# Eight retention units ahead of the first gated product, with its weights prepared in small steps

## The chip, the cores and the metric

The kernel runs on one core of a Trainium2 chip. The core has five engines that follow their own instruction streams in order and wait for each other through semaphores: TensorE (PE, matmuls, whose weight loads are listed as PEld), VectorE (DVE), ScalarE (ACT), GpSimd (POOL) and SyncE (SP, which issues all DMAs here). The metric is the device time of one execution in microseconds; each program was timed in several runs and the median counts. One further execution was taken with the hardware profiler, and all rows below are from that one.

## What is computed

Retention (attention with a decaying mask, no softmax) over 8 batches, 8 heads and 576 positions, then two feed-forward layers on the 4608 tokens.

```python
def _attn_ref(q, k, v):                        # (8, 8, 576, 64)
    scores = scale * np.matmul(q, k.transpose(0, 1, 3, 2))
    Dmat = np.where(rel >= 0, gamma[:, None, None] ** rel[None, :, :], 0.0)
    ret = scores * Dmat[None, :, :, :]
    return np.matmul(ret, v)

def _moe_ref(x, w_in, w_out):                  # 512 -> 2048 -> 512
    h = x @ w_in
    g = h * np.cos(h)
    return g @ w_out

def _moe2_ref(x, w1, w2, w3, w_out):           # 512 -> 768 -> 512
    h = np.maximum(np.maximum(x @ w1, x @ w2), x @ w3)
    return h @ w_out
```

## The kernel before

The tokens are cut into 9 blocks of 512 (`NBLK`), the heads into 4 pairs (`NPAIR`), so retention has 36 units, numbered n = 4 x block + pair; a tile `u1_2` belongs to block 1, pair 2, unit 6. A unit loads 1 MB of q, k and v (`att_load`), scales v on POOL (`att_scale`), multiplies q and k on PE (`att_scores`, `sc`, 16 small matmuls), masks the scores on DVE (`att_mask`), adds k and v products to a running state in PSUM (`att_state`, one matmul for each chunk of up to 128 positions), copies the state to SBUF on ACT before each of them (`att_keep`), forms the output on PE from masked scores and copied states (`att_out`, `po`), and decays it on DVE into the block's quarters `k1`, `k2` (`att_decay`). All pairs keep their state in one PSUM bank, so a state matmul follows the last copy out of that bank.

The matrix products use a seven-product scheme on quarters of the matrices, and each operand is split in a high and a low part: seven products of 12 matmuls take the place of eight. `build_in` prepares a block's seven operands `x_x` (differences of quarters, the high part as a cast on ACT, the low part as a subtraction on DVE). A group (`group_in`) does the seven products (`d_a`, `b_a`, `sums` are its PSUM banks) for two weight pairs; its last product is written after four products of the next group. The result goes through `gate` (h cos h) on ACT and DVE. In the first phase each block has two groups, with weight pairs 0 and 1, then 2 and 3; a second phase does the other half with operands stored to DRAM and loaded again as `x_y`.

Weights come as 64-bit floats. For each pair the raw halves are loaded, `widen` (ACT, two activations a half) and `join` (DVE, two instructions a half) build the single-precision value, `total` (POOL) adds its two parts to `fa`, `sums` (DVE, four instructions) forms differences of quarters, `piece_high` casts on ACT and `piece_low` subtracts on DVE. `lead_in` does this for pairs 0 to 3 in the opening: five steps, one a slot, both halves in one step, the sums and all casts of a pair in the fourth (`add_up`, with `split_pair`). `background` prepares later pairs the same way.

What sets the order is a hand-made agenda. `at(n, fn)` puts a step n slots ahead; `tick()` writes all steps of the current slot, in the order in which they were put there, and goes to the next. Each product of a group ends with a tick, so in the gated phase a slot is one product plus the steps due. The opening runs 15 slots without products (lines 733 to 747). The first five units start two slots apart there (scores at the start, one state step in each following slot, output in the fifth, decay in the sixth); pair 0 starts in slot 0, pair 1 in slot 2, pairs 2 and 3 in slots 12 and 15. From the first product on, a unit starts every 3.5 slots (`start_of`). Every engine executes in written order, and a DMA is written to SP's stream where `at` puts it.

## Time and profile before

| | us |
|---|---|
| median of three runs (lowest, highest) | 1456.78 (1455.54, 1458.35) |
| the profiled execution | 1458.0 |
| span of its instructions | 1456.2 |
| PE busy | 1416.6 (97%) |
| DVE busy | 1166.9 (80%) |
| ACT busy | 779.5 (54%) |
| POOL busy | 177.2 (12%) |

The page gives busy times of the whole span. Where an engine is the bound in one stage and not in another, the windows by stage show it: for each stretch the busy time of each engine with its number of instructions, the clock that was granted to PE as a share of full speed, and the mean busy share of the 16 DMA engines. The timeline lists an engine's instructions in order, equal ones that follow each other in one row, with start, duration, and in square brackets the idle time before the row and what ended it.

### The profile page before, as it was taken

The numbers are of one execution on the slowest core, as the hardware profiler recorded it, in microseconds if no ns is written. First come the engines' busy times: TensorE is split into PE (matmuls) and PEld (weight loads), VectorE is DVE, ScalarE is ACT, GpSimd is POOL, SyncE is SP. The second block draws the span as 40 slices with busy tenths as digits, with TensorE's granted clock in tenths as the row PEclk, the third lists the DMA queues.
The fourth block names the chain that finished last, engine by engine and source line by source line (L and its number), as shares of the span: only waits on it lengthen the run. The fifth ranks groups of instructions, "written<-read, shape, count | busy, mean of one in ns | idle before, by whom it ended". The sixth has DMA issues, their size and how long they took to land.

```text
span 1456.2 us, 26320 instructions
## 1 busy us (share of the span) xinstructions
PE 1416.6 (97%) x10492; PEld 1300.9 (89%) x10492; DVE 1166.9 (80%) x1649; ACT 779.5 (54%) x1259; POOL 177.2 (12%) x128
## 2 busy tenths in 40 slices
PE   7799999999899998999999999999999999999998
PEld 5688888998899998999999999998888888888887
DVE  6877888889887679999999999677676667868875
ACT  3566655666788776454444444344343434545543
POOL 2243343442021000000000000000000000000000
PEclk9999999999999999999999999999999999999999
DMA  7588898996999885456556656923344294535633
GB/s 304 176 286 293 316 309 286 335 329 231 359 379 375 325 301 202 143 184 209 195 190 224 223 185 257 369 72 124 98 147 146 73 348 179 181 117 173 227 121 116
DMA packets 95034, 331.52 MB, mean 228 GB/s; under 512 B 9408, under 2 KB 17600, under 8 KB 88768
## 3 DMA queue, kind: packets, MB, share of 16 engines
q1 hardware_dynamic: 94912, 329.85, 63.9%
q8 instruction: 82, 1.34, 0.4%
q14 instruction: 40, 0.33, 0.1%
HBM read 197.69 MB, written 132.12 MB: 226 GB/s over the span
## 4 chain that ended last, share of the span: by engine, by line
PE 90%; DVE 4%; DMA 2%; ACT 1%; issue 1%; POOL 0%; SPq 0%; POOLq 0%; DVEq 0%; ACTq 0%
PE wo L853 24%; PE d_a L394 13%; PE d_e L415 13%; PE b_e L415 6%; PE b_a L394 6%; PE d_u L1255 4%; PE a_e L415 3%; PE sums L394 3%; PE state L597 3%; PE po L613 3%; PE sc L554 2%; PE b_u L1255 2%; PE po L625 2%; PE d_b L394 2%; DMA x_y<-xs 1%; PE a_u L1255 1%
## 5 line engine op out<-in xcount | busy, mean ns | idle before, releaser
L853 PE MATMUL wo<-h_g,w_wo 128*128 128x256 f32 x1728 | 312.8, 283 | 0.0
L853 PEld LDWEIGHTS wo<-h_g,w_wo 128*128 128x128 f32 x1728 | 269.5, 192 | 0.0
L853 PE MATMUL wo<-l_g,w_wo 128*128 128x256 f32 x864 | 245.1, 284 | 4.6 <-DVE l_g L826 4.5
L853 PEld LDWEIGHTS wo<-l_g,w_wo 128*128 128x128 f32 x864 | 165.8, 192 | 5.6 <-DVE l_g L826 5.4
L394 PE MATMUL d_a<-x_x,w_wi 128*128 128x256 f32 x864 | 120.6, 290 | 1.9 <-DVE x_x L373 1.9
L510 DVE SCALAR_TENSOR_TENSOR s_a<-t_a,s_a 128x1024 f32<-128x1024 f32 x72 | 95.2, 1322 | 28.2 <-ACT t_a L507 28.2
L415 PE MATMUL d_e<-h_e,w_b 128*128 128x512 f32 x432 | 115.5, 389 | 0.0
L394 PEld LDWEIGHTS d_a<-x_x,w_wi 128*128 128x128 f32 x864 | 108.7, 193 | 5.7 <-DVE x_x L373 2.1
L394 PE MATMUL d_a<-x_y,w_wi 128*128 128x256 f32 x864 | 111.6, 285 | 2.1 <-DMA x_y<-xs 2.0
L821 ACT CAST h_g<-tb_g 128x1024 fp32r<-128x1024 f32 x36 | 37.8, 1051 | 139.5 <-DVE tb_g L365 139.5
L394 PEld LDWEIGHTS d_a<-x_y,w_wi 128*128 128x128 f32 x864 | 107.7, 194 | 2.5 <-ACT ar_wo L174 2.1
L440 ACT ACTIVATE ext<-d_e 128x512 f32<-128x512 f32 x72 | 43.0, 597 | 118.2 <-PE d_e L415 117.8
L501 DVE SCALAR_TENSOR_TENSOR t_a<-s_a,t_a 128x1024 f32<-128x1024 f32 x72 | 92.0, 1278 | 17.6 <-ACT t_a L497 17.4
L507 ACT ACTIVATE t_a<-t_a 128x1024 f32<-128x1024 f32 x72 | 76.1, 1056 | 40.0 <-DVE t_a L501 39.8
L415 PEld LDWEIGHTS d_e<-h_e,w_b 128*128 128x128 f32 x432 | 81.0, 188 | 16.8
L186 POOL TENSOR_TENSOR fa_b<-raw_b 128x512 uint32<-128x512 uint32 x18 | 22.2, 1231 | 537.1 <-DVE raw_b L180 499.4
L497 ACT ACTIVATE t_a<-s_a 128x1024 int32<-128x1024 f32 x72 | 76.1, 1057 | 2.1 <-PE d_a L394 1.4
L597 PE MATMUL state<-u 128*128 128x128 f32 (+1 forms) x256 | 56.5, 309 | 15.8 <-ACT u L581 10.9
L444 DVE TENSOR_TENSOR ext<-ext,b_e 128x512 f32<-128x512 f32 x36 | 24.7, 685 | 57.4 <-PE b_e L415 57.4
L581 ACT COPY u<-state 128x128 f32<-128x128 f32 x128 | 32.4, 266 | 67.6 <-PE state L597 67.4
L415 PE MATMUL d_e<-l_e,w_b 128*128 128x512 f32 x216 | 66.5, 389 | 0.0
L597 PEld LDWEIGHTS state<-u 128*128 128x128 f32 (+1 forms) x256 | 39.8, 197 | 25.3 <-issue 11.5
(268 smaller groups left out, 3281.7 us busy)
## 6 DMA issues: line engine op xcount, KB each, us to landing
u<-att SPq DMA_DIRECT2D x36, 1024.0 KB, 8.1
gq<-s_a SPq DMA_DIRECT2D x72, 512.0 KB, 6.9
k_g<-gq SPq DMA_DIRECT2D x72, 512.0 KB, 6.1
xs<-x_x SPq DMA_DIRECT2D x63, 512.0 KB, 8.3
x_y<-xs SPq DMA_DIRECT2D x63, 512.0 KB, 7.5
w_b<-st_b SPq DMA_DIRECT2D x9, 1792.0 KB, 10.7
st_b<-p_b SPq DMA_DIRECT2D x27, 512.0 KB, 4.7
mqp<-ext SPq DMA_DIRECT2D x24, 512.0 KB, 3.1
```

Source lines behind the costliest of these rows:

```text
L394: nc.tensor.matmul(h[:, p * HB : (p + 1) * HB], a, b, start=first and p == 0 and i == 0, stop=i == len(terms) - 1, skip_group_check=True,)
L415: nc.tensor.matmul(dst, a, b, start=first and i == 0, stop=i == len(terms) - 1, skip_group_check=True)
L440: nc.scalar.activation(dst, b[:, :n], AF.Copy, scale=scale)
L497: nc.scalar.activation(st["t"], s, AF.Copy, bias=0.25)
L501: nc.vector.scalar_tensor_tensor(out=r, in0=s, scalar=MOST_TURNS, in1=st["t"], op0=ALU.min, op1=ALU.subtract)
L507: nc.scalar.activation(r, r, AF.Sin, scale=TURN, bias=HALF_PI)
L510: nc.vector.scalar_tensor_tensor(out=s, in0=f32(st["t"]), scalar=-1.0, in1=s, op0=ALU.max, op1=ALU.mult)
L597: nc.tensor.matmul(state[:, hp * CH : (hp + 1) * CH], kn[p : p + m, sl], v[p : p + m, sl], start=False, stop=True, skip_group_check=True,)
L613: nc.tensor.matmul(po[64 * e : 64 * e + 64, s * CH : (s + 1) * CH], v[:, s * CH + 64 * e : s * CH + 64 * e + 64], u["ret"][:, e, s * CH : ...
L821: nc.scalar.copy(h, o[pairs[k][2]])
L853: nc.tensor.matmul(b[:, mt * HB : (mt + 1) * HB], a, v, start=first and mt == 0 and p == 0 and i == 0, stop=last and p == len(ws) - 1 and ...
L1255: nc.tensor.matmul(dst, a, v, start=first and p == 0 and i == 0 and (wide or mt == 0), stop=p == 2 and i == 2, skip_group_check=True,)
```

## The change

Eight units instead of five are started ahead of the first product, two slots apart from slot 1, and the opening runs 17 slots (`LEAD`). From then on a unit starts every 3.75 slots. `at` takes a flag, and steps with it (scores and outputs) are written ahead of the other steps of their slot, so ahead of the state matmuls. The steps of a weight pair are eleven instead of five: each half is widened, joined and totalled by itself, the sums stand alone, and high and low pieces come in two parts each; the list `EARLY` gives their slots (the first pieces are cast a slot before the sums, which they don't need). Pairs 0 to 3 start in slots 0, 3, 12 and 16. Unit 0 is loaded ahead of the first raw weights, and units 0 to 3 and the raw weights of pairs 0 and 1 are asked for at once; the raw weights of pairs 2 and 3 are loaded by halves in slots 8, 9, 11 and 12. The operands of block 0 are built one slot later, in slots 10 and 14; those of the other blocks keep their slots.

```diff
-    def at(n, fn):
-        agenda.setdefault(slot[0] + n, []).append(fn)
+    def at(n, fn, ahead=False):
+        due = agenda.setdefault(slot[0] + n, [[], []])
+        due[0 if ahead else 1].append(fn)
 
     def tick():
-        due = agenda.setdefault(slot[0], [])
-        while due:
-            due.pop(0)()
+        due = agenda.setdefault(slot[0], [[], []])
+        while due[0] or due[1]:
+            (due[0] or due[1]).pop(0)()
...
-        at(start, lambda: att_scores(n))
+        at(start, lambda: att_scores(n), True)
         at(start, lambda: att_keep(n, 0))
...
-        at(start + 5, lambda: att_out(n))
+        at(start + 5, lambda: att_out(n), True)
         at(start + 6, lambda: att_decay(n))
...
-    first_load(0)
     att_load(0)
+    first_load(0, 0)
+    first_load(0, 1)
     att_load(1)
-    first_load(1)
+    first_load(1, 0)
+    first_load(1, 1)
     att_load(2)
-
-    def first_steps(i):
+    att_load(3)
+    def lead_in(i, start, join_on, sum_on, steps):
         st = lead[i]
...
-            sums("wi", st["fa"], st["s"], nc.vector)
-            st["lows"] = split_pair("wi", i, st["fa"], st["s"])
-
-        return [widen_both, join_both, total_both, add_up, lambda: st["lows"]()]
-
-    def lead_in(i, start):
-        for k, fn in enumerate(first_steps(i)):
+            sums("wi", st["fa"], st["s"], sum_on)
+
+        fns = [
+            lambda: widen_half(0),
+            lambda: join(st["raw", 0], st["t"][:, 0], join_on),
+            lambda: total_half(0),
+            lambda: widen_half(1),
+            lambda: join(st["raw", 1], st["t"][:, 1], join_on),
+            lambda: total_half(1),
+            add_up,
+            *split,
+        ]
+        for k, fn in zip(steps, fns):
             at(start + k, fn)
...
-    at(3, lambda: first_load(2))
-    at(4, lambda: att_load(3))
-    at(5, lambda: first_load(3))
-    at(6, lambda: att_load(4))
-    at(9, lambda: att_load(5))
-    lead_in(0, 0)
-    at(2, lambda: lead_in(1, 0))
-    for n in range(5):
-        att_unit(n, 2 * n)
-    for i, n in ((2, 12), (3, 15)):
-        at(n, lambda i=i: lead_in(i, 0))
-    build_in(block_of(0), 9, 13, xsd[0], nc.vector)
-    for _ in range(15):
+    NLEAD = 8
+    LEAD = 17
+    EARLY = (0, 1, 2, 1, 2, 3, 4, 3, 4, 5, 6)
+    for n in range(4, NLEAD + 2):
+        at(2 * n - 5, lambda n=n: att_load(n))
+    for i, n in ((2, 8), (3, 11)):
+        for p in range(2):
+            at(n + p, lambda i=i, p=p: first_load(i, p))
+    lead_in(0, 0, nc.vector, nc.vector, EARLY)
+    at(3, lambda: lead_in(1, 0, nc.vector, nc.vector, EARLY))
+    for n in range(NLEAD):
+        att_unit(n, 2 * n + 1)
+    at(12, lambda: lead_in(2, 0, nc.vector, nc.vector, EARLY))
+    at(16, lambda: lead_in(3, 0, nc.vector, nc.vector, EARLY))
+    build_in(block_of(0), 10, 14, xsd[0], nc.vector)
+    for _ in range(LEAD):
         tick()
 
-    def start_of(k):
-        return max(3 * (k - 1), 0) if k < 3 else (7 * k - 11) // 2
-
-    for k in range(1, NUNIT - 4):
-        if k > 1:
-            at(max(0, start_of(k) - 4), lambda k=k: att_load(4 + k))
-        att_unit(4 + k, start_of(k))
+    def start_of(n):
+        return (15 * (n - NLEAD)) // 4
+
+    for n in range(NLEAD, NUNIT):
+        if n >= NLEAD + 2:
+            at(max(0, start_of(n) - 4), lambda n=n: att_load(n))
+        att_unit(n, start_of(n))
```

Three places show what stands where. First PE in the lead-in, around the output of unit 1 (`po1`); `state_154` is the state's bank, `u0_1` to `u0_3` and `u1_0` are the tiles of units 1 to 4. Before:

```order
L613 MATMUL po1_325<-u0_1_165 64x128 x8
L625 MATMUL po1_325<-u0_1_165 64x128 x6
L597 MATMUL state_154<-u0_2_171 128x128
L597 MATMUL state_154<-u0_3_243 128x128
L597 MATMUL state_154<-u0_2_171 128x128
L597 MATMUL state_154<-u0_3_243 128x128
L554 MATMUL sc4_0_354<-u1_0_301 128x128
```

After:

```order
L598 MATMUL state_154<-u0_1_165 128x128
L598 MATMUL state_154<-u0_2_171 128x128
L614 MATMUL po1_317<-u0_1_165 64x128 x8
L626 MATMUL po1_317<-u0_1_165 64x128 x6
L598 MATMUL state_154<-u0_2_171 128x128
L598 MATMUL state_154<-u0_3_173 128x128
L555 MATMUL sc4_0_343<-u1_0_212 128x128
```

Four state matmuls in a row became two and two, with an output or scores between the pairs.

Second PE around the first gated products, where `d_a0_0`, `b_a0_0` and `sums` are the banks of block 0, group 0, `w_wi0` and `w_wi1` the two weight pairs. Before:

```order
L625 MATMUL po4_435<-u1_0_301 64x64 x2
L394 MATMUL d_a0_0_472<-x_x0_0_391,w_wi0_227 128x256 x6
L394 MATMUL d_a0_0_472<-x_x0_0_391,w_wi1_296 128x256 x6
L554 MATMUL sc5_0_501<-u1_1_366 128x128
```

After:

```order
L626 MATMUL po5_538<-u1_1_251 64x64 x2
L598 MATMUL state_154<-u1_1_251 128x128
L598 MATMUL state_154<-u1_2_300 128x128
L395 MATMUL d_a0_0_575<-x_x0_0_392,w_wi0_215 128x256 x6
L395 MATMUL d_a0_0_575<-x_x0_0_392,w_wi1_287 128x256 x6
L555 MATMUL sc8_0_590<-u2_0_404 128x128
```

The first product has five units' outputs and no scores beyond them ahead of it before, and six outputs and eight units' scores now.

Third ACT around the second half of pair 2's casts, with the copies of the state that PE waits for. Before:

```order
L203 CAST w_wi2_495<-fa_wi2_469 128x2x256
L207 ACTIVATE w_wi2_495<-fa_wi2_469 128x256
L210 CAST w_wi2_495<-s_wi2_490 128x2x256 x2
L581 COPY u1_1_366<-state_154 128x128
L583 ACTIVATE state_154<-cs_152 128x128
```

After:

```order
L204 CAST w_wi2_535<-fa_wi2_505 128x2x256
L208 ACTIVATE w_wi2_535<-fa_wi2_505 128x256
L582 COPY u1_2_300<-state_154 128x128
...
L370 CAST x_x0_6_611<-k2_x0_408 128x512
L211 CAST w_wi2_535<-s_wi2_565 128x2x256 x2
L175 ACTIVATE t_wi3_572<-raw_wi3_0_406 128x512
```

The casts that read the sums (`s_wi2`) moved away from the first ones, and copies stand between.

## Rows read from the trace of the kernel before

**Rows 1.** The page: busy time of each engine over the whole span.

```profile
PE 1416.6 (97%) x10492; PEld 1300.9 (89%) x10492; DVE 1166.9 (80%) x1649; ACT 779.5 (54%) x1259; POOL 177.2 (12%) x128
```

**Rows 2.** Windows: stretch, PE, PEld, DVE, ACT, POOL busy (instructions), clock, DMA share, GB/s.

```profile
0.00:42.80 42.80, 31.79 (x269) 23.59 (x269) 28.89 (x60) 17.34 (x41) 10.29 (x14) 1.00 0.70 282
42.80:60.00 17.20, 13.06 (x106) 12.05 (x105) 17.06 (x30) 11.10 (x25) 8.55 (x7) 0.90 0.67 249
60.00:80.00 20.00, 16.54 (x164) 14.52 (x163) 15.89 (x35) 7.68 (x19) 4.05 (x4) 0.91 0.50 145
300.00:350.00 50.00, 50.00 (x509) 46.61 (x509) 41.88 (x73) 32.13 (x65) 13.75 (x10) 1.00 0.77 278
350.00:400.00 50.00, 43.11 (x333) 41.45 (x333) 43.85 (x61) 37.37 (x59) 6.35 (x4) 0.97 0.90 330
```

**Rows 3.** Timeline of PE in the lead-in: start, duration, instruction [idle before <-releaser].

```profile
20.38 2.08 PE L554 MATMUL sc<-u 64*128 64x128 f32 x16
...
27.26 1.16 PE L554 MATMUL sc<-u 64*128 64x128 f32 x16
28.35 1.09 PE L613 MATMUL po<-u 128*64 128x128 f32 x16
...
30.18 0.49 PE L597 MATMUL state<-u 128*128 128x128 f32 x2
31.11 0.46 PE L597 MATMUL state<-u 128*128 128x128 f32 x2 [0.45 <-ACT u L581]
31.93 0.71 PE L597 MATMUL state<-u 128*128 128x128 f32 x4 [0.35 <-ACT u L581]
32.57 1.16 PE L554 MATMUL sc<-u 64*128 64x128 f32 x16
```

**Rows 4.** Timeline of PE in the first two gated groups.

```profile
51.69 0.77 PE L597 MATMUL state<-u 128*128 128x128 f32 x2 [2.92 <-ACT state L583]
52.10 2.73 PE L394 MATMUL d_a<-x_x,w_wi 128*128 128x256 f32 x12
...
63.67 0.48 PE L597 MATMUL state<-u 64*128 64x128 f32 x2 [2.75 <-ACT u L581]
64.08 1.40 PE L613 MATMUL po<-u 128*64 128x128 f32 x16
...
70.61 1.68 PE L394 MATMUL b_a<-x_x,w_wi 128*128 128x256 f32 x12
```

**Rows 5.** Timeline of ACT at the second casts of weight pair 2.

```profile
49.78 1.29 ACT L210 CAST w_wi<-s_wi 128x512 fp32r<-128x512 f32 x2 [3.38 <-DVE s_wi L194]
```

**Rows 6.** Window of DVE alone, from pair 0's sums to pair 3's last pieces.

```profile
15.03:66.30 51.27, 48.40 (x96) 0.95 0.55 215
```

**Rows 7.** Window of 5 us, columns as in rows 2, around PE's first long wait.

```profile
50.00:55.00 5.00, 3.14 (x14) 2.97 (x14) 4.96 (x13) 4.92 (x11) 0.00 (x0) 0.66 0.74 292
```

**Rows 8.** Timeline of POOL: the scaling of unit 2.

```profile
17.02 1.05 POOL L542 TENSOR_TENSOR u<-u,cs 128x512 f32<-128x512 f32 x1 [2.02 <-DMA u<-att]
```

**Rows 9.** Timeline of DVE: two low parts, a mask and a decay.

```profile
45.97 1.53 DVE L373 TENSOR_TENSOR x_x<-k_x,x_x 128x512 fp32r<-128x512 f32 x1
...
53.07 1.41 DVE L563 TENSOR_TENSOR u<-sc,cs 128x384 f32<-128x384 f32 x4
...
57.24 0.68 DVE L373 TENSOR_TENSOR x_x<-k_x,x_x 128x512 fp32r<-128x512 f32 x1
...
67.94 1.24 DVE L640 SCALAR_TENSOR_TENSOR k_x<-po,cs 128x64 f32<-128x64 f32 x5
```

**Rows 10.** Timeline of POOL beside the first and the last of rows 9.

```profile
45.41 2.99 POOL L542 TENSOR_TENSOR u<-u,cs 128x512 f32<-128x512 f32 x2
...
67.55 1.04 POOL L186 TENSOR_TENSOR ar_wi<-ar_wi 128x512 uint32<-128x512 uint32 x1 [7.27 <-PE po L625]
```

**Rows 11.** Timeline of PE at the turn to the second phase.

```profile
385.08 4.86 PE L394 MATMUL d_a<-x_y,w_wi 128*128 128x256 f32 x24 [1.96 <-DMA x_y<-xs]
```

**Rows 12.** Window at the same turn, columns as in rows 2.

```profile
370.00:380.00 10.00, 8.77 (x72) 8.39 (x71) 9.57 (x15) 7.04 (x12) 0.00 (x0) 1.00 1.00 351
```

More of the change, by code (lines that the diff above doesn't have):

```diff
@@ L175, in widen, with join @@
         nc.scalar.activation(low, low, AF.Copy, scale=2.0**-29)
-    def join(raw, t):
+    def join(raw, t, eng=nc.vector):
         high = raw.rearrange("p (n t) -> p n t", t=2)[:, :, 1]
-        nc.vector.tensor_scalar(out=t, in0=t, scalar1=3, scalar2=None, op0=ALU.logical_shift_left)
-        nc.vector.scalar_tensor_tensor(
+        eng.tensor_scalar(out=t, in0=t, scalar1=3, scalar2=None, op0=ALU.logical_shift_left)
+        eng.scalar_tensor_tensor(
             out=high, in0=high, scalar=0x80000000, in1=t, op0=ALU.bitwise_and, op1=ALU.bitwise_or
@@ L298, in high @@
         def high(k):
-            st["src", k] = piece_high(kind, st["fa"], st["s"], k, piece(k))
+            st["src", k] = piece_high(kind, st["fa"], st.get("s"), k, piece(k))
         def low(k):
@@ L671, in retention_ffn, with first_load @@
     lead = {}
-    def first_load(i):
-        st = lead[i] = {}
-        st["raw"] = [x4(f"raw_wi{i}_{n}", [2 * NB], U32) for n in range(2)]
-        for n in range(2):
-            load_raw(st["raw"][n], "wi", i, n)
-    first_load(0)
+    def first_load(i, n):
+        st = lead.setdefault(i, {})
+        st["raw", n] = x4(f"raw_wi{i}_{n}", [2 * NB], U32)
+        load_raw(st["raw", n], "wi", i, n)
     att_load(0)
+    first_load(0, 0)
+    first_load(0, 1)
     att_load(1)
-    first_load(1)
+    first_load(1, 0)
@@ L683, in retention_ffn, with widen_half, total_half @@
+    first_load(1, 1)
     att_load(2)
-    def first_steps(i):
+    att_load(3)
+    def lead_in(i, start, join_on, sum_on, steps):
         st = lead[i]
-        def widen_both():
-            st["t"] = x4(f"t_wi{i}", [2, NB], U32)
-            for n in range(2):
-                widen(st["raw"][n], st["t"][:, n])
-        def join_both():
-            for n in range(2):
-                join(st["raw"][n], st["t"][:, n])
-        def total_both():
-            st["fa"] = x4(f"fa_wi{i}", [4, HB])
-            for n in range(2):
-                total(st["raw"][n], st["fa"][:, 2 * n : 2 * n + 2].rearrange("p q n -> p (q n)"), nc.gpsimd)
+        split = split_steps("wi", i, st)
+        def widen_half(n):
+            if "t" not in st:
+                st["t"] = x4(f"t_wi{i}", [2, NB], U32)
+            widen(st["raw", n], st["t"][:, n])
+        def total_half(n):
+            if "fa" not in st:
+                st["fa"] = x4(f"fa_wi{i}", [4, HB])
+            total(st["raw", n], st["fa"][:, 2 * n : 2 * n + 2].rearrange("p q n -> p (q n)"), nc.gpsimd)
@@ L731, in block_of @@
         return quarters_of.setdefault(j, {"name": f"x{j}", "n": NB})
[L733 to L755 removed]
+    NLEAD = 8
[14 more added lines that the diff above has]
+    for _ in range(LEAD):
+        tick()
+    def start_of(n):
[4 more added lines that the diff above has]
+        att_unit(n, start_of(n))
     for j in range(1, NBLK):
[L757 to L758 removed]
+        build_in(block_of(j), 14 * j - 9, 14 * j - 2, xsd[j], nc.gpsimd)
     back = [(k, i) for k, n in (("wi", 4), ("wo", 0), ("b", 0), ("o", 0)) for i in range(n, len(PAIRS[k]))]
```

2 lines of the change are left out of this document (removed).

## The prediction, made before the changed kernel was run

> **What bounds the kernel now.** I read the page's busy shares first [rows 1]: PE is busy for 1416.6 of 1456.2 us, so whatever the change does to the other engines, it can win at most the 39.6 us in which PE is idle, and some of the time in which PE runs slowly. Next the windows by stage [rows 2] tell where the idle time lies: 11.0 us before 42.8, 4.1 us from there to 60, 3.5 us to 80, none from 300 to 350 and 6.9 us from 350 to 400. The diff moves retention units and weight steps in the opening, so the 18.6 us of the first 80 us are what it can reach; later, until 350, PE is the bound and its work is unchanged.
>
> The opening has two stages. In the lead-in PE loses time to loads and then in small pieces: a state matmul waits for the copy that ScalarE (ACT) takes of the state, 0.45 and 0.35 us in each unit [rows 3]. In the second stage, up to 70.61, the pieces are large, 2.92 and 2.75 us, both ahead of a state matmul [rows 4]. ACT's row shows why [rows 5]: the two casts of a weight pair waited 3.38 us for VectorE's sums, and the copy that PE needs stands behind them. VectorE (DVE) is the late one: it works 17.06 of 17.2 us [rows 2], and 48.40 of the 51.27 us from the first sums to the last weight pieces [rows 6]. Around PE's first long wait the granted clock is 0.66 in a 5 us slice, a stretch at 1.2 instead of 2.4 GHz [rows 7]: 12 product matmuls take 2.73 us at 52.10 but 1.68 at 70.61, the first part of an output 1.40 at 64.08 but 1.09 at 28.35 [rows 3, 4].
>
> **The change, part by part.** I compare the two programs at one point, the second product of the second gated group (b_a, at 70.61 in the profile [rows 4]), because it needs the last prepared weights. Up to there the changed order has the same products, and on top scores of 2 units, outputs of 3, and 11 state matmuls. Prices are distances between starts: scores 27.26 to 28.35, 1.09 us; outputs 28.35 to 30.18, 1.83 us [rows 3]; a state matmul 63.67 to 64.08, 0.41 us [rows 4]. That is 2.2 + 5.5 + 4.5 = 12.2 us of PE work that is already done when this point is reached. The gain is 12.2 us less however much later than 70.61 the point now comes.
>
> PE's way to that point. (1) Loads: unit 0 is now queued ahead of the two raw weights, but unit 2 stays the eighth transfer and the bytes ahead of it are the same, so I expect its data at 17.0, where POOL's scaling ends its wait for it [rows 8]. Today its scores start at 20.38 [rows 3], since more state matmuls stand ahead. Now three state matmuls and their copies stand ahead, and I put the scores at 17.8. With 2.08 us for scores at the lower clock [rows 3], four states at up to twice their price (some 3 us) and an output (1.83, some of it slow), the scores of unit 3 come at about 25, against 27.26 today. (2) A unit takes 5.31 us there now (27.26 to 32.57), 0.80 of it the two waits for copies. In the new order scores or an output stand between a copy and the next state matmul in one of the two places; in the other, two state matmuls of different units still follow each other with a copy between. So a period of 4.96 us, and four of them to unit 7's scores: 44.8. Its scores, an output, four states and one wait take 1.1 + 1.8 + 1.6 + 0.45, 5.0 us: the first product starts at 49.8. (3) From there to b_a stand seven products at 1.64 (b_a's 1.68 less the overlap of two), two scores, three outputs and eleven states, 11.5 + 2.2 + 5.5 + 4.5 = 23.7 us, and six slots with one 0.45 us wait each plus 0.7 us in all for ACT's longer queue, 3.4 us: b_a at 76.9.
>
> DVE's way to that point. From the first sums to the last weight pieces it has today's 48.40 us [rows 6], and now three more masks at up to 1.41, three more decays at 1.24 and three more instructions of 512 columns (a join's two, an addition) at 0.68 [rows 9]: 4.2 + 3.7 + 2.0 = 9.9 us. GpSimd (POOL) runs five more instructions in that time; a DVE instruction of 512 columns took 1.53 instead of 0.68 us when POOL ran beside it [rows 9, 10], and I let half of the five meet one: 2 us. Started at 14 to 15 us, DVE is ready at 74 to 75 if it never waits, and at 78 with the 2.9 us that it waited today. So PE's way and DVE's way end within some 2 us of each other, at 76 to 78; I take 77.0. The opening gains 12.2 - 6.4 = 5.8 us.
>
> The smaller weight steps change who waits for whom. Today a late sum holds, on ACT, every copy queued behind the pair's casts. Now the second casts stand a slot after the sums, and PE has a product and an output or scores (2.7 to 3.5 us) as cover. If DVE is later than that cover, the long waits return at pairs 2 and 3, for up to the 2.92 and 2.75 us of today.
>
> SP's queue: raw weights of pairs 2 and 3 are loaded in halves behind units 6 to 9, and those loads wait for an earlier unit's output on PE. They are asked for three or more slots of 2.5 us ahead, and the DMA share is 0.67 and 0.50 in the second stage [rows 2], so I cost this at nothing; 0 to 3 us are its bounds, the upper one a long wait of [rows 4].
>
> Steady stage and tail. Units now come every 3.75 slots instead of 3.5, the last one ends two slots earlier, and PE does the same work without idle time [rows 2]: 0, within two or three 0.45 us waits either way. In the tail PE is already idle for 6.9 us [rows 2], 1.96 of it at one load [rows 11], and two more slots run without retention as cover: 0 to 1.5 us of loss. I take 0.
>
> **Sum.** Against the profiled execution's 1458.0 us (its span of 1456.2 and 1.8 around it): 1452.2. The median of the three runs is 1456.78, 1.2 below that execution; the result is such a median, so 1456.8 - 5.8 = 1451.0.
>
> **Rivals.** First, the gain is given back at the turn to the second phase. From 370 to 380 the DMA share is 1.00 and DVE works 9.57 of 10 us [rows 12], and at 385 PE waits for x_y [rows 11]. If bytes or DVE, not PE, set when that turn comes, PE arrives earlier and waits: 5.8 us back, 1456.8. Against: the DMA share is 0.77 from 300 to 350 [rows 2], and the moved loads come earlier too.
>
> Second, slower: DVE falls behind in the opening because masks and decays of three more units stand ahead of the last weight pieces. Some 20 POOL instructions run until b_a; if each held a DVE instruction for 0.85 us [rows 9, 10], DVE would need 17 us more, less some 4 us that today's 48.40 already hold: instead of 75 it is ready at 88. This decides from 70.6 + 12.2 = 82.8 on; 88 is 5 us slower, 1462. Against: masks and decays, which read PSUM, are most of what is added, and the decay at 67.94 took its 1.24 us with POOL at work from 67.55 [rows 9, 10], so its price holds that already. The Trainium skill (SBUF — State Buffer, Who interferes with whom) says that a DVE instruction with two SBUF inputs and a POOL instruction that reads SBUF exclude each other, and that one with at most one SBUF input does not contend; rows 9 agree in the first, and by the rule at its hardest the sum is this rival's.
>
> Third, the waits all go: the loads alone bound the opening, PE idle for some 6.7 us up to 17.8 and not after. Idle time up to b_a today is 11.0 + 4.1 + 2.75 us [rows 2, 4] and slow rows cost about 2.9 more (1.05 for the product, 0.31 for an output's first part, the rest the same way), so the gain would be near 14 us, 1443. Against it: DVE's way alone ends at 74.
>
> Fourth, waits stay: 0.35 us more in each of four periods and one long wait at a pair, 4 us less gain, 1455.
>
> **How the numbers follow.** Forecast, with 3 to 9 us of gain: 0.66, 1451.0. Everything gone: 0.06, 1443. Given back at the turn: 0.12, 1456.8. Waits stay: 0.08, 1455. DVE late: 0.08, 1462. A measurement of this kernel tells 0.2%, 2.9 us, from no change. Faster is 0.66 + 0.06 = 0.72, the same 0.12 + 0.08 = 0.20, slower 0.08. The range goes down to 1446 (10.8 us: 5.8, 2 where DVE and POOL don't meet, 3 where the six slots have no waits) and up through the cases of no change to 1457.5.
>
> **What would show it.** Right: the first product at 49 to 51 us; b_a of the second group at 76 to 78; no slice after 25 us with a granted clock below 0.9; PE waits for state copies of at most 1 us; 13 to 15 us of PE idle time in the first 80 instead of 18.6. Wrong: a wait of over 2 us behind the casts of pairs 2 or 3, or b_a waiting for the last weight piece (DVE late); the opening as said but over 9 us idle from 350 to 400 (given back); new stalls between 100 and 350.

## The result and the profile after

| | us |
|---|---|
| before, median of four runs (lowest, highest) | 1457.49 (1455.54, 1458.35) |
| changed, median of four runs (lowest, highest) | 1442.43 (1441.91, 1442.90) |
| ratio, 95% interval | 0.9899 (0.9887 to 0.9912) |
| profiled execution: span before, after | 1456.2, 1440.9 |

The kernel became 15 us faster. The direction was forecast, the size was not: the forecast was 1451.0 with a range from 1446.0 to 1457.5, and the time lies below the range.

The page's busy times of the whole span, against [rows 1], then the windows, against [rows 2], with two short stretches of the opening added (columns as there):

```profile
PE 1412.6 (98%) x10492; PEld 1298.7 (90%) x10492; DVE 1165.2 (81%) x1649; ACT 778.9 (54%) x1259; POOL 174.2 (12%) x128
```

```profile
0.00:42.80 42.80, 33.53 (x308) 25.45 (x310) 32.94 (x70) 18.65 (x46) 15.20 (x17) 0.88 0.91 349
42.80:60.00 17.20, 15.31 (x164) 13.41 (x162) 17.10 (x40) 12.18 (x31) 6.76 (x6) 1.00 0.53 205
60.00:80.00 20.00, 20.00 (x219) 18.24 (x219) 16.81 (x34) 9.41 (x22) 3.86 (x4) 1.00 0.74 246
...
50.00:55.00 5.00, 4.35 (x52) 3.62 (x50) 4.97 (x12) 3.86 (x11) 1.27 (x1) 1.00 0.39 156
15.00:20.00 5.00, 4.21 (x23) 3.50 (x24) 4.93 (x11) 3.87 (x9) 1.75 (x2) 0.50 1.01 421
```

PE is busy for 4.0 us less and idle for 28.3 instead of 39.6 us. Less busy time for the same matmuls comes at least in part from fewer slow rows: the stretch from 50 to 55, at a granted clock of 0.66 before [rows 7], has 1.00 now, and the opening is slow only between 10 and 25 us, with 0.50, a clock of 1.2 GHz, from 15 to 20. Ahead of 42.8 us the clocks of the two profiles can't be compared: before, 1.00 is recorded there [rows 2], though scores took 2.08 us at 20.38 [rows 3], as long as those at 17.28 below, in the stretch with 0.50. In the 37.2 us from 42.8 to 80 PE idles for 1.9 us instead of 7.6. DVE still works nearly all of 42.8 to 60.

The timeline of PE, in the opening and then at the first x_y product, with which the turn to the second phase begins; the last block shows where the turn began before:

```profile
12.05 2.08 PE L555 MATMUL sc<-u 64*128 64x128 f32 x16 [2.26 <-DMA u<-att]
...
17.28 2.08 PE L555 MATMUL sc<-u 64*128 64x128 f32 x16
...
24.31 1.16 PE L555 MATMUL sc<-u 64*128 64x128 f32 x16
...
29.19 1.16 PE L555 MATMUL sc<-u 64*128 64x128 f32 x16
...
33.17 1.16 PE L555 MATMUL sc<-u 64*128 64x128 f32 x16
...
42.52 1.16 PE L555 MATMUL sc<-u 64*128 64x128 f32 x16
...
47.44 1.68 PE L395 MATMUL d_a<-x_x,w_wi 128*128 128x256 f32 x12
...
51.07 0.46 PE L598 MATMUL state<-u 128*128 128x128 f32 x2 [0.45 <-ACT u L582]
...
55.08 0.91 PE L598 MATMUL state<-u 64*128 64x128 f32 x4 [0.28 <-ACT state L584]
...
58.35 0.46 PE L598 MATMUL state<-u 128*128 128x128 f32 x2 [0.71 <-ACT u L582]
...
63.56 1.68 PE L395 MATMUL b_a<-x_x,w_wi 128*128 128x256 f32 x12
65.08 0.39 PE L598 MATMUL state<-u 128*128 128x128 f32 x2
65.22 1.68 PE L395 MATMUL d_a<-x_x,w_wi 128*128 128x256 f32 x12
...
70.55 1.79 PE L395 MATMUL b_a<-x_x,w_wi 128*128 128x256 f32 x12
...
357.39 1.60 PE L395 MATMUL d_a<-x_y,w_wi 128*128 128x256 f32 x12
...
369.70 4.92 PE L395 MATMUL d_a<-x_y,w_wi 128*128 128x256 f32 x24 [2.20 <-DMA x_y<-xs]
```

```profile
372.62 1.60 PE L394 MATMUL d_a<-x_y,w_wi 128*128 128x256 f32 x12
```

The second product of the second gated group, b_a, the point at which the prediction compares the kernels, starts at 70.55, where it started at 70.61 before [rows 4], with 12.2 us of retention work more behind it. Between the first product and b_a PE waits 0.45, 0.28 and 0.71 us for copies; before it waited 2.92, 1.23 and 2.75. The turn comes 15.2 us earlier (it began at 372.62), and from there both kernels take the same time (1083.5 and 1083.6 us): the wait at 369.70 is the one of [rows 11], 2.20 instead of 1.96. So 12.2 us were won up to b_a and 3.0 between b_a and the turn. The price of 12.2 us is borne out: from b_a to the turn PE is busy for 283.0 us where it was 295.1, 12.1 us less.

The timeline of ACT at the second casts of pairs 2 and 3 (of [rows 5]), that of DVE at an add of the gated result (`plus` in `group_in`) and at the last pieces of pair 3, and the window of DVE alone from pair 0's sums to these pieces (of [rows 6]):

```profile
52.25 1.14 ACT L211 CAST w_wi<-s_wi 128x512 fp32r<-128x512 f32 x2
...
65.65 1.13 ACT L211 CAST w_wi<-s_wi 128x512 fp32r<-128x512 f32 x2
```

```profile
65.35 0.69 DVE L447 SCALAR_TENSOR_TENSOR s_a<-b_a,s_a 128x512 f32<-128x512 f32 x1 [1.48 <-PE b_a L395]
...
69.97 2.78 DVE L220 TENSOR_TENSOR w_wi<-s_wi,w_wi 128x512 fp32r<-128x512 f32 x2
```

```profile
14.14:72.75 58.61, 56.59 (x122) 0.93 0.74 271
```

The casts no longer wait for DVE's sums (3.38 us before). DVE ends its pieces 6 us later than before and idles for only 2.0 us on the way, 1.48 of them at 65.35, where its add waits for PE's product. b_a takes 1.79 instead of 1.68 us, probably since its second half meets the first of these pieces: PE and DVE arrive together, but DVE's last steps stand behind a product of PE.

### The profile page after: what moved, and what is told of

The parts are those of the page before. It is cut to its first block, busy times and chain, and to the rows that moved or that the text cites. A ratio compares the mean times of both kernels' runs of the same rounds, so it can differ in the third digit from the quotient of the medians.

```text
span 1440.9 us, 26303 instructions
## 1 busy us (share of the span) xinstructions
PE 1412.6 (98%) x10492; PEld 1298.7 (90%) x10492; DVE 1165.2 (81%) x1649; ACT 778.9 (54%) x1259; POOL 174.2 (12%) x128
## 4 chain that ended last, share of the span: by engine, by line
PE 71%; DVE 2%; DMA 1%; ACT 1%; issue 0%; DVEq 0%
PE wo L860 24%; PE d_e L416 14%; PE b_e L416 7%; PE d_a L395 6%; PE d_u L1262 5%; PE a_e L416 3%; PE b_a L395 3%; PE b_u L1262 2%; PE sums L395 2%; PE d_b L395 2%; PE a_u L1262 1%; PE b_b L395 1%; DMA x_y<-xs 1%; PE d_u_single L1262 1%; PE a_b L395 0%
## 5 line engine op out<-in xcount | busy, mean ns | idle before, releaser
L502 DVE SCALAR_TENSOR_TENSOR t_a<-s_a,t_a 128x1024 f32<-128x1024 f32 x72 | 93.5, 1298 | 17.9 <-ACT t_a L498 17.7
L395 PE MATMUL b_a<-x_x,w_wi 128*128 128x256 f32 x432 | 59.8, 288 | 0.0
```

The costliest lines, as they stand in the source:

```text
L395: nc.tensor.matmul(h[:, p * HB : (p + 1) * HB], a, b, start=first and p == 0 and i == 0, stop=i == len(terms) - 1, skip_group_check=True,)
L502: nc.vector.scalar_tensor_tensor(out=r, in0=s, scalar=MOST_TURNS, in1=st["t"], op0=ALU.min, op1=ALU.subtract)
```

## Experiments: three parts

The change can be cut in three: the eight units (with their loads, the 17 slots and 3.75 slots a unit), the small weight steps, and scores and outputs ahead in their slot ("order"). Three theories stood at the start, each crediting most of the gain to one part: A to the units as work under which waits hide, B to the small steps, C to the order. The first four runs leave one or two parts out of the change or add one to the kernel before.

**e1_no_ahead**: the change without the order.

```diff
-        at(start, lambda: att_scores(n), True)
+        at(start, lambda: att_scores(n))
...
-        at(start + 5, lambda: att_out(n), True)
+        at(start + 5, lambda: att_out(n))
```

> The changed kernel with scores and outputs written in their old place, behind the state steps of the slot; eight units and small weight steps stay. Theory A (the units that stand ahead give PE work while DVE prepares weights; the order within a slot only hides copies): one or two 0.45 us waits for a copy come back in each of the seven units of the lead-in and one in each slot of the first group, 3 to 5 us, so 1445 to 1448 us, 9 to 12 us faster than the kernel before. Theory B (small weight steps are what frees PE): the same 1445 to 1448. Theory C (the order within the slot is what frees PE): most of the gain is lost, 1451 or more.

**e2_coarse**: the change with five coarse steps a weight pair.

```diff
-            lambda: widen_half(0),
-            lambda: join(st["raw", 0], st["t"][:, 0], join_on),
...
+            lambda: (widen_half(0), widen_half(1)),
+            lambda: [join(st["raw", n], st["t"][:, n], join_on) for n in range(2)],
+            lambda: (total_half(0), total_half(1)),
+            lambda: (add_up(), split[0](), split[2]()),
+            lambda: (split[1](), split[3]()),
...
+    EARLY = (0, 1, 2, 3, 4)
```

> The changed kernel with the weight steps of before: five steps a pair, both halves in one step, all casts of a pair in the slot of its sums; eight units and the order within a slot stay. Theory A: the casts that wait for DVE's sums hold a copy again at pairs 2 and 3, but PE has scores and outputs ahead of the state matmul: 1 to 3 us slower than the changed kernel, 1443.5 to 1446 us. Theory B: the two long waits of before, 2.9 and 2.75 us, and the slow clock after them come back, 6 us or more: 1448 to 1452. Theory C: as A.

**e3_ahead_only**: the kernel before with the order alone (with the flag of `at` and `tick` as in the change).

```diff
-        at(start, lambda: att_scores(n))
+        at(start, lambda: att_scores(n), True)
...
-        at(start + 5, lambda: att_out(n))
+        at(start + 5, lambda: att_out(n), True)
```

> The kernel before with one edit: scores and outputs are written ahead of the other steps of their slot. Theory A: 1 to 3 us faster than before (the 0.45 us waits in the lead-in), 1454 to 1456; the long waits behind the casts stay. Theory B: the same. Theory C: 6 us or more faster, 1451 or less.

**e6_eight_only**: the edits of e1_no_ahead and e2_coarse together, so that only the eight units are left.

> The changed kernel without the order within a slot and without the small steps: eight units ahead, the loads moved, a unit every 3.75 slots. Theory A: 8 to 12 us faster than before, 1445 to 1449, since three units' work now stands where PE waited. Theory B: at most 5 us faster, 1452 or more, since the casts still wait behind DVE's sums. Theory C: at most 5 us faster.

Measured, against runs of before on the same chip: e1 0.9950 (0.9934 to 0.9966), e2 0.9941 (0.9922 to 0.9960), e3 0.9980 (0.9970 to 0.9989), e6 1.0011 (0.9999 to 1.0022). Theory A fell: eight units alone gain nothing. Neither do B or C hold alone; the times of e1 (1448.63), e2 (1446.50) and e3 (1453.21) lie in no theory's range. The order gives 3 us by itself and 7 as the last part (e1 against the changed kernel), the small steps 6 as the last part (e2). PE's rows in e6_eight_only show why, first one line of its waits up to b_a (us in total, times, longest), then the timeline of PE, then ACT's at the same place:

```profile
PE state L598 <- ACT u L582: 15.9, 16, 3.4
```

```profile
44.77 0.46 PE L598 MATMUL state<-u 128*128 128x128 f32 x2 [2.52 <-ACT u L582]
45.16 1.87 PE L555 MATMUL sc<-u 64*128 64x128 f32 x16
...
59.72 0.46 PE L598 MATMUL state<-u 128*128 128x128 f32 x2 [2.28 <-ACT u L582]
...
81.15 1.68 PE L395 MATMUL b_a<-x_x,w_wi 128*128 128x256 f32 x12
```

```profile
42.12 0.68 ACT L175 ACTIVATE t_wi<-raw_wi 128x512 f32<-128x512 f32 x1
42.69 0.67 ACT L176 ACTIVATE raw_wi<-raw_wi 128x512 uint32<-128x512 uint32 x1
43.26 0.65 ACT L175 ACTIVATE t_wi<-raw_wi 128x512 f32<-128x512 f32 x1
43.81 0.66 ACT L176 ACTIVATE raw_wi<-raw_wi 128x512 uint32<-128x512 uint32 x1
44.37 0.25 ACT L582 COPY u<-state 128x128 f32<-128x128 f32 x1
```

A copy of the state stands on ACT behind the four activations that widen both halves of a pair, 2.3 us in a row, and PE stands at the state matmul that needs it, with scores queued behind that could have run. More units bring more state matmuls, so more places where this can happen: b_a comes 10.5 us later than before and of the 12.2 us of extra work 1.7 are won. In the changed kernel a half's two activations stand in one step, not a pair's four, and scores or an output ahead of the state matmul fill the time. The prediction had seen such a hold only at the casts.

## Experiments: five units, and a theory that fell

**e5_small_only** and **e4_five_units**: the kernel before with small steps (the change's `lead_in`), without and with the order.

```diff
-    lead_in(0, 0)
-    at(2, lambda: lead_in(1, 0))
+    EARLY = (0, 1, 2, 1, 2, 3, 4, 3, 4, 5, 6)
+    lead_in(0, 0, nc.vector, nc.vector, EARLY)
+    at(2, lambda: lead_in(1, 0, nc.vector, nc.vector, EARLY))
```

> The kernel before with the small weight steps alone. Theory D (DVE is the limit with five units): b_a of the second group at 67 to 70.6, 1453 to 1456 us. Rival S (parts add up): the waits of 2.92 and 2.75 us at pairs 2 and 3 and the slow clock behind them go, b_a at 64 to 65, 1450 to 1451 us.

> The kernel before (five units ahead, its loads, 3.5 slots a unit) with the small weight steps and with scores and outputs ahead. Theory D: with five units DVE sets when the last weight pieces are there (48.4 us busy of 51.3, and with order alone the second group's b_a came at 67.9, right behind the last pieces at 67.1), so taking PE's waits away gains little more: b_a at 66 to 69 and 1452 to 1454 us, about as with order alone (1453.2). Rival S: the parts add up (about 3 us for order, 6 for small steps): b_a at 62 to 64, 1447 to 1449 us.

Measured: e5 1.0002 (0.9992 to 1.0011), e4 0.9997 (0.9987 to 1.0008). Neither gains anything; that is nearer to theory D than to S, though D's times were too low for both (1456.82 for 1452 to 1454 in e4, 1458.21 for 1453 to 1456 in e5). The timelines of PE and of DVE in e4_five_units show the wait that D names:

```profile
62.67 0.98 PE L395 MATMUL d_a<-x_x,w_wi 128*128 128x256 f32 x6 [1.33 <-DVE w_wi L220]
...
68.58 1.65 PE L395 MATMUL b_a<-x_x,w_wi 128*128 128x256 f32 x6 [3.99 <-DVE w_wi L220]
```

```profile
67.01 3.18 DVE L220 TENSOR_TENSOR w_wi<-s_wi,w_wi 128x512 fp32r<-128x512 f32 x2
```

But a late piece can be late for two reasons: DVE has no time, or the piece stands too far back in its order. The small steps end six slots after their start, the coarse ones four, and the kernel before starts pairs 2 and 3 only three slots and no slot ahead of the first product; the change starts them five slots and one slot ahead. That had been hidden in the part "eight units". Four runs take it apart.

**e15_five_early** is e4_five_units with the earlier start, **e17_coarse_early** is e3_ahead_only with it, **e18_small_early** is e5_small_only with it; **e16_pairs_late** takes it from the changed kernel.

```diff
-    for i, n in ((2, 12), (3, 15)):
+    for i, n in ((2, 10), (3, 14)):
```

```diff
-    at(12, lambda: lead_in(2, 0, nc.vector, nc.vector, EARLY))
-    at(16, lambda: lead_in(3, 0, nc.vector, nc.vector, EARLY))
+    at(14, lambda: lead_in(2, 0, nc.vector, nc.vector, EARLY))
...
     for _ in range(LEAD):
         tick()
+    lead_in(3, 0, nc.vector, nc.vector, EARLY)
```

> Five units with small steps and with scores and outputs ahead, as in the run with all but the eight units, but weight pairs 2 and 3 start in slots 10 and 14 of the 15, so as far ahead of the first product as in the changed kernel (5 and 1 slots instead of 3 and 0). Theory D (with five units DVE has no time, whatever its order): the wait for the last pieces goes, and waits for other work of DVE (operands, sums) take its place; b_a of the second group ends at 69 to 72 us, 1453 to 1457 us. Rival T (the small steps end two slots later than the coarse ones, and in a 15 slot opening that alone was too late): b_a ends at 65 to 67 us, 1446 to 1450 us.

> The changed kernel with pairs 2 and 3 started three slots and no slot ahead of the first product (slots 14 and 17), as the kernel before does, instead of five and one. Rival T: the last pieces come a slot or two later in DVE's order, behind a mask, a decay and gate steps (some 4 us), and b_a of the second group waits for them: it ends 3 to 5 us later, 1445.5 to 1447.5 us. Theory D without T (only the amount of DVE's work counts, not its order): b_a ends within 1.5 us of 72.3, 1442 to 1444 us.

> Five units, scores and outputs ahead, coarse weight steps as before, but pairs 2 and 3 start in slots 10 and 14 instead of 12 and 15. Theory E (the early start is what counts, the size of the steps is not): b_a of the second group ends at 65 to 66.5 us as with small steps, 1449 to 1451 us. Rival G (the size of the steps counts too: the coarse casts still wait on ACT for DVE's sums and hold the copies of the state): a wait of 2 to 3 us stays at each of pairs 2 and 3, b_a ends at 67.5 to 69.6 us, 1452 to 1454 us.

> Five units, small weight steps with pairs 2 and 3 in slots 10 and 14, but scores and outputs in the old order. Theory E (start counts): the opening gains nearly as with the order (b_a of the second group ends at 65 to 67 us), 1449.5 to 1452 us. Rival O (the order is needed: it was worth 2.7 us of the opening by itself): b_a ends at 67.5 to 70 us, 1452.5 to 1455 us.

Measured: e15 0.9955 (0.9938 to 0.9971), e16 0.9908 (0.9893 to 0.9923), e17 1.0001 (0.9992 to 1.0011), e18 0.9991 (0.9981 to 1.0000). Theory D fell for five units: with the earlier start they gain 7 us, and b_a ends at 64.9, 7.4 us earlier than before. DVE had the time, the order of its work was wrong. In e16 b_a waits 2.23 us for the pieces and ends 2.1 us later, between what T and D said; the time, 1443.37 us, is within D's, and its interval overlaps the changed kernel's. With eight units the start matters less, as PE itself comes late to b_a. G and O hold and E fell: the early start needs the small steps (e17, slower even than G said) and the order (e18). In e17 it is ACT again, whose casts wait for the sums at both pairs, as they did before (3.38 us at pair 2 [rows 5], 1.78 at pair 3), and PE waits for an operand of DVE; the timelines of ACT and of PE:

```profile
46.01 1.29 ACT L211 CAST w_wi<-s_wi 128x512 fp32r<-128x512 f32 x2 [1.99 <-DVE s_wi L195]
...
59.32 1.29 ACT L211 CAST w_wi<-s_wi 128x512 fp32r<-128x512 f32 x2 [2.77 <-DVE s_wi L195]
```

```profile
55.25 1.21 PE L395 MATMUL d_a<-x_x,w_wi 128*128 128x256 f32 x8 [2.75 <-DVE x_x L374]
```

All kernels of these two sections side by side; PE's idle time is the sum of its rows up to the second group's b_a, the end of b_a is its last row's start and duration, and the eight-unit kernels have 12.2 us of work more behind them there. The times are those of the one profiled execution, the ratio is of all runs; e1's profiled execution took 1453.67 us, 5 us above its median, so its turn is later than its ratio tells:

| kernel | units | pairs 2, 3 | steps | order | PE idle | b_a ends | turn | ratio |
|---|---|---|---|---|---|---|---|---|
| before | 5 | late | coarse | old | 17.9 | 72.3 | 372.6 | 1 |
| e3 | 5 | late | coarse | ahead | 16.5 | 69.6 | 369.0 | 0.9980 |
| e5 | 5 | late | small | old | 17.5 | 71.5 | 372.6 | 1.0002 |
| e4 | 5 | late | small | ahead | 17.8 | 70.2 | 370.6 | 0.9997 |
| e17 | 5 | early | coarse | ahead | 20.3 | 73.7 | 373.5 | 1.0001 |
| e18 | 5 | early | small | old | 16.6 | 69.1 | 369.4 | 0.9991 |
| e15 | 5 | early | small | ahead | 14.1 | 64.9 | 364.5 | 0.9955 |
| e6 | 8 | early | coarse | old | 21.0 | 82.8 | 371.6 | 1.0011 |
| e1 | 8 | early | small | old | 15.6 | 76.7 | 367.1 | 0.9950 |
| e2 | 8 | early | coarse | ahead | 14.9 | 76.6 | 362.5 | 0.9941 |
| after | 8 | early | small | ahead | 11.2 | 72.3 | 357.4 | 0.9899 |

Read from e15 to after, the eight units with all that came with them are worth 8 us: 12.2 less the 7.4 by which b_a ends later, 4.8, in the opening, and the rest behind it. With them came the loads, the wider spacing (below), and two shifts of operands that were not tried alone. Block 0's are built seven and three slots ahead of the first product, where the five-unit kernels have six and two. Block 1's first one is begun five slots behind the first product instead of seven, so not all other blocks keep their slots: its first difference on POOL came at 59.03 us, where it came at 74.95 before. The gain of the eight units needs the other parts, as that of the small steps needs the early start.

## Experiments: what else bounds the opening, and the spacing

**e9_masks_twice** and **e10_sums_pool** load and unload DVE in the opening of the changed kernel.

```diff
         at(start + 1, lambda: att_mask(n))
+        if 4 <= n < 8:
+            at(start + 1, lambda: att_mask(n))
```

```diff
-    at(12, lambda: lead_in(2, 0, nc.vector, nc.vector, EARLY))
+    at(12, lambda: lead_in(2, 0, nc.vector, nc.gpsimd, EARLY))
```

(the same for pair 3)

> The changed kernel with the masks of units 4 to 7 done twice: four more masks of 1.41 us on DVE between 25 and 50 us, 5.6 us in all, none of it needed. Theory D (in the opening DVE has no slack, PE and DVE reach pair 3 together): DVE's idle time after 20 us takes up to 1.5 us of it, the last weight pieces come 4 to 5.6 us later, b_a of the second group waits for them, 1445.5 to 1448 us. Rival (PE alone bounds the changed opening, DVE has slack): b_a within 1 us of 70.55, 1442.4 us within 1.

> The changed kernel with the sums of pairs 2 and 3 on POOL instead of DVE: 2.9 us less for DVE in the opening (four instructions of 0.41 to 0.43 us for each pair, 1.46 us from the first start to the last end of the starts). Theory D in its balanced form (DVE and PE come together, b_a holds a wait of only 0.1 us): next to nothing to gain, 1441.5 to 1443.5 us. Rival (DVE alone is the bound there): b_a 2 to 3 us earlier, 1439.5 to 1440.5 us.

Measured: e9 0.9928 (0.9914 to 0.9943), 1446.16 us; e10 0.9905 (0.9891 to 0.9920), 1442.74 us. DVE has little slack in the changed opening: of 5.6 us added, b_a ends 3.9 us later (76.28 instead of 72.34), and the time grows by about as much. The 1.48 us in which DVE waited for PE at 65.35 are used up, and the last pieces start at 73.93 instead of 69.97. PE comes late by then too: it waits 1.40 us for a copy and 0.54 for a mask around 52, its rows are slow there (a clock of 0.65 and 0.66 from 50 to 60 us), and only 0.37 us of wait is left at the piece. So DVE is not alone in front: with the sums gone from it b_a comes no earlier (70.71): PE's way is as long as without it, and the add that stands ahead of the last pieces waits longer for PE's product. The timeline of DVE in e10_sums_pool:

```profile
65.52 0.69 DVE L447 SCALAR_TENSOR_TENSOR s_a<-b_a,s_a 128x512 f32<-128x512 f32 x1 [2.26 <-PE b_a L395]
```

Part of the relief is also given back, by rows of DVE at pair 2's first piece, e10_sums_pool first, the changed kernel second:

```profile
48.31 1.52 DVE L220 TENSOR_TENSOR w_wi<-fa_wi,w_wi 128x512 fp32r<-128x512 f32 x1
```

```profile
49.34 0.68 DVE L220 TENSOR_TENSOR w_wi<-fa_wi,w_wi 128x512 fp32r<-128x512 f32 x1
```

The first runs beside POOL, which is busy until 49.3 with the work that the sums pushed back. The Trainium skill (SBUF — State Buffer, Who interferes with whom) states that a DVE instruction with two SBUF inputs contends with a POOL instruction that reads SBUF; the 1.52 against 0.68 us agree.

**e13_seven**: seven units in 15 slots, pairs 2 and 3 five slots and one slot ahead of the first product, their loads two slots earlier, 3.6 slots a unit; the operands of block 0 stay in slots 10 and 14.

```diff
-    NLEAD = 8
-    LEAD = 17
+    NLEAD = 7
+    LEAD = 15
```

> Seven units ahead in 15 slots instead of eight in 17, pairs 2 and 3 two slots earlier, 3.6 slots a unit behind. Theory D: pair 3 is ready on DVE at 70 to 72 us, as with five units (70.2) and with eight (72.8), and PE has one unit, 4.1 us, less to do until then, so b_a or the product before it waits 2 to 4 us for DVE, and the tail loses some of the wider spacing: 1445 to 1448 us. Rival (seven are cover enough): no wait for DVE at pairs 2 and 3 over 0.5 us, 1442 to 1443.5 us.

Measured: 0.9973 (0.9963 to 0.9982), 1453.16 us. The direction of D holds, the loss against the changed kernel, 11 us, is twice the most that it said. What waits is not the weight piece but products that need two other operands of DVE, x_x, for 1.83 us at 55.27 and 1.92 at 65.63. The edit puts these operands two slots nearer to their products than in the changed kernel: they stayed in their slots while the first product moved from slot 17 to 15. The timelines of PE and of DVE in e13_seven show what that does at the second wait:

```profile
65.63 1.64 PE L395 MATMUL d_a<-x_x,w_wi 128*128 128x256 f32 x8 [1.92 <-DVE x_x L374]
```

```profile
63.13 0.69 DVE L447 SCALAR_TENSOR_TENSOR s_a<-b_a,s_a 128x512 f32<-128x512 f32 x1 [3.96 <-PE b_a L395]
```

DVE stands idle for 3.96 us with an add that needs PE's product before (b_a, at 61.33), and the operand that this product needs stands behind the add, at 64.89. So at this wait it is DVE's order again, not its amount of work. Whether both waits go when the operands move along was not run, and this run does not tell what the eighth unit is worth by itself. The turn comes 11.7 us later than in the changed kernel: b_a ends 1.8 us later with a unit's work, 4.1 us, less behind it, 3.6 are longer waits from there to the turn (7.4 instead of 3.8), and the rest was not taken apart; the spacing, next, is part of it.

**e7_spacing** and **e14_wider**: the changed kernel with 3.5 and 3.85 slots a unit.

```diff
-        return (15 * (n - NLEAD)) // 4
+        return (7 * (n - NLEAD)) // 2
```

```diff
-        return (15 * (n - NLEAD)) // 4
+        return (77 * (n - NLEAD)) // 20
```

> The changed kernel, but units start every 3.5 slots instead of 3.75 once the products run. Theory: of the some 3 us that the changed kernel gained behind the opening, half lies ahead of the turn (PE waits of 3.3 us before, 1.8 after) and comes from the wider spacing, so this loses 1.5 to 3 us: 1444 to 1445.5 us. Rival: spacing does nothing, order within the slots does: 1442.4 us within 1.

> The changed kernel with units 3.85 slots apart behind the opening instead of 3.75, so that the last one ends two slots later. With 3.5 the last output came 46 us ahead of the turn and PE waited 4.72 us for DVE there, with 3.75 it came 29 us ahead. Theory (retention is the cover of the slots and lacks at the end): the wait of 0.54 us for DVE at 340 goes, perhaps more: 1441 to 1442.4 us. Rival (the last units now come too late for the operands of the last block, or too close to its gates): a new wait of 1 to 3 us ahead of the turn, 1443.5 to 1446 us.

Measured: e7 0.9965 (0.9952 to 0.9977), 1451.52 us; e14 0.9918 (0.9904 to 0.9933), 1444.61 us. Both miss their theories, e7 by far: with eight units ahead the spacing is worth 9 us, not 1.5 to 3. In e14 the rival holds, with its time and with its wait. The opening of e7 is the changed kernel's (b_a at 69.42); the loss comes later. The timelines of PE and of ACT in e7_spacing, then its windows (columns as in [rows 2]):

```profile
319.92 1.09 PE L626 MATMUL po<-u 64*64 64x128 f32 x16
...
345.03 2.93 PE L395 MATMUL sums<-x_x,w_wi 128*128 128x256 f32 x12 [4.72 <-ACT sums L464]
```

```profile
339.36 1.06 ACT L508 ACTIVATE t_a<-t_a 128x1024 f32<-128x1024 f32 x1 [4.61 <-DVE t_a L502]
```

```profile
320.00:345.00 25.00, 20.18 (x172) 19.60 (x172) 22.37 (x30) 16.18 (x27) 5.52 (x3) 0.98 0.54 211
...
343.00:348.00 5.00, 2.97 (x14) 2.97 (x15) 4.45 (x6) 3.53 (x5) 0.00 (x0) 0.61 0.68 274
348.00:353.00 5.00, 5.00 (x33) 5.00 (x33) 2.19 (x5) 3.55 (x7) 0.00 (x0) 0.71 0.72 269
```

With eight units ahead and the old rate, the last output starts 46 us ahead of the turn (at 319.92 of 366.25); in the kernel before it started 28 (at 344.39), in the changed one 29 us ahead of it (at 328.06). In the slots that are left PE has products only, DVE has a whole slot's gate and operand work, 22.4 of 25 us, and falls behind: ACT waits 4.61 us for it with the copy that PE needs queued behind, PE stands for 4.72 us, and the clock falls. Of the 10.0 us by which the stretch from b_a to the turn grew, 4.0 are such waits ahead of the turn (5.75 us where the changed kernel has 1.78) and 2.6 slow rows behind them (2.93 for 1.68 and 4.41 for 3.04); another 3.1 are longer waits between 83 and 199 us, nearly all for copies (5.09 us where it has 2.02). The 3.75 slots spread the units that are left over the same products. At 3.85 the old wait of 1.86 us for DVE, which the changed kernel had cut to 0.54, is back ahead of the turn (342.45). So 3.75 lies between two losses.

**e8_ahead_lead**: the order for the eight units of the opening alone.

```diff
-        at(start, lambda: att_scores(n), True)
+        at(start, lambda: att_scores(n), n < NLEAD)
...
-        at(start + 5, lambda: att_out(n), True)
+        at(start + 5, lambda: att_out(n), n < NLEAD)
```

> The changed kernel, but scores and outputs stand ahead only for the eight units of the opening; from unit 8 on in the old order. Theory: the order counts later too (without it a wait of 1.69 us at 88 and one of 1.77 at 298 with a slow clock behind it were there): 1445 to 1448 us, opening as in the changed kernel (b_a of the second group within 1 us of 70.55). Rival: the order counts in the opening only: 1442.4 us within 1.

Measured: 0.9909 (0.9895 to 0.9924), 1444.15 us, between the two expectations; the interval overlaps the changed kernel's, so this run does not settle it. Its profile has the wait that was expected at 88, at 84.08 (1.69 instead of 0.60 us), and a turn at 360.03 instead of 357.39. No kernel of these runs is measurably faster than the changed one.

## Why the prediction was wrong in size

**Right.** The bound (PE, most of whose idle time within reach lay in the opening), the point of comparison, the 12.2 us of work ahead, the loads: scores of unit 2 were forecast at 17.8 and came at 17.28, and the last scores to the first product took 4.9 us where 5.0 were said. From the turn on nothing changed, as said.

**The step that failed** is PE's way from the scores of unit 3 to b_a, which was put too long by 6.4 us: 77.0 against 70.55. Its terms:
- the scores of unit 3: 25 against 24.31, 0.7 us
- four periods of 4.96 us to unit 7's scores, 19.8 us: they took 18.2 (24.31 to 42.52). Two of the four took 3.98 us (29.19 to 33.17, and on to 37.15), with three state matmuls in them instead of four and no wait for a copy.
- from the first product to b_a 27.1 us: they took 23.1. The waits were put at 3.4 us and are 1.44. I had taken one wait of 0.45 us a slot and 0.7 for ACT's queue; with a product in front, a copy is mostly done when PE comes to its state matmul. The work was put at 23.7 us and took 21.7. By distances between starts, less the waits, 1.5 of these 2.0 us are the eleven state matmuls (3.0 for 4.5) and 0.5 the products (10.95 for 11.5). Each state matmul was priced at 0.41 us, a distance between starts from a place where PE had just waited [rows 4]. Behind a product it is nearly free: b_a starts at 63.56, a state matmul at 65.08 and the next product at 65.22, 1.66 us for both, where 1.64 had been put for the product alone.

DVE's way was put at 74 to 78 and ended at 72.75: 56.59 us of work where 60.3 (48.4 + 9.9 + 2) had been priced. Of the 58.61 us up to there, 1.48 are the wait for PE's product at 65.35, so DVE's end followed PE's in part. How far a further cut of PE's way would have met DVE was not tried.

**Steady stage and tail, put at 0,** gave 3.0 us: PE's waits between b_a and the tail went from 3.55 us (five of 0.71) to 2.02 (0.60, 0.45, 0.26 and 0.71), those of the tail ahead of the turn from 3.32 (0.22, 1.86 and 1.24) to 1.78 (0.54 and 1.24). The prediction had looked for idle time from 300 to 350 us, where PE has none [rows 2]; the five waits of 0.71 stood between 73 and 232. It held that two more slots without retention at the end would cost up to 1.5 us. The step looked at the slots and not at the time: the last output now starts 29 us ahead of the turn, where it started 28 before. Together 5.8 forecast + 6.4 + 3.0 = 15.2, the 15.3 us of the two spans.

**The rivals.** "Given back at the turn" didn't happen here, but it does when the spacing is left at 3.5: e7_spacing loses 10 us between b_a and the turn (296.8 us instead of 286.8), some 6.6 of them where DVE is late and 3.1 in longer waits for copies; none of PE's waits there is for a DMA. "DVE late" didn't happen either, but a later start (2.23 us of wait for the pieces, e16) or five units with late pairs (3.99 us, e4) bring it about; 5.6 us of masks (e9) make PE and DVE late alike and leave 0.37 us of wait at the piece. "The waits all go", at 1443 with a chance of 0.06, has the nearest time, but for another reason: 3.5 us of waits stayed between 17.8 us and b_a, the opening gave 12.2 and not 14, and the rest came from the stage that was put at 0. "Waits stay" was wrong.

**The signs named ahead:** a clock of 1.00 from 25 us up to the turn, and copies of the state waited for at most 0.73 us, came as said; the first product (47.44 for 49 to 51), b_a (70.55 for 76 to 78) and the idle time in the first 80 us (11.2 for 13 to 15) were all better than said.

**Left open:** the order of the first loads was not tried alone, what the order gives from unit 8 on is not settled (e8), nor what seven units lose when the operands move with them (e13). What the shifts of block 0's and block 1's operands cost or give was not tried.

## What to carry to other kernels

Parts of a schedule change can be worth little or nothing alone and 15 us together (ratios 1.0011, 1.0002 and 0.9980 alone, 0.9899 for the whole): an earlier start, finer steps and independent work ahead of the waiting instruction each move the wait to the next engine in the row until all are there. Work that is pulled ahead leaves a gap where it was; stretch the rate of what is left, or the gap becomes a wait near the end. Price an instruction from a place where its neighbours are those of the new order, not behind a wait.

## What the chip showed unexpectedly

Waits of the same length had different effects on the granted clock. In e1_no_ahead PE waited 1.69 us at 88.14 and 1.77 us at 297.90 for the same kind of copy; around the first the clock stayed at 1.00, behind the second it fell to 1.2 GHz for some rows. Windows of e1_no_ahead:

```profile
295.00:300.00 5.00, 3.23 (x34) 2.73 (x34) 5.00 (x5) 2.23 (x4) 3.11 (x2) 0.93 0.96 376
300.00:305.00 5.00, 5.00 (x41) 4.88 (x38) 3.87 (x9) 2.50 (x5) 0.00 (x0) 0.73 1.03 338
85.00:90.00 5.00, 3.31 (x34) 2.87 (x33) 3.22 (x4) 4.94 (x9) 4.12 (x3) 1.00 0.35 141
90.00:95.00 5.00, 5.00 (x56) 4.52 (x55) 5.00 (x10) 1.28 (x3) 3.59 (x3) 1.00 0.71 241
```

The same pair of low pieces on DVE (two instructions of 512 columns) took 1.28 us at pair 1, 2.13 at pair 2 and 2.78 at pair 3 in the changed kernel, and 3.18 in e4_five_units; POOL was at work beside the longer ones.
